# Eight more attention items with float32 score operands in an attention, gated-product and soft mixture-of-experts kernel

## The chip, the cores and the metric

The kernel runs on one core of a Trainium2 chip. The metric is the time of one execution on the device in microseconds (us), the median of three runs. The engines are TensorE (PE in the profile; its weight loads are PEld), VectorE (DVE), ScalarE (ACT), GpSimd (POOL) and SyncE (SP), which here only issues transfers.

## The reference

Three stages follow each other: causal attention with a learned decay, a product of two linear maps with two more linear maps behind it, and a soft mixture of eight experts. The change touches the first one alone, and there the line with `np.matmul(q, k...)` and the decay `bias`.

```python
batch, n_heads, seq, head_dim = (4, 8, 576, 64)
...
    scores = scale * np.matmul(q, k.transpose(0, 1, 3, 2))
    causal = np.triu(np.ones((S, S), dtype=bool), k=1)
    s_pos = np.maximum(s, 0.0)
    cum = np.cumsum(s_pos, axis=-1)
    bias = -(cum[:, :, :, None] - cum[:, :, None, :])
    scores = np.where(causal, -1000000000.0, scores + np.minimum(bias, 0.0))
    scores = scores - np.max(scores, axis=-1, keepdims=True)
    attn = np.exp(scores)
    attn = attn / (np.sum(attn, axis=-1, keepdims=True) + 1e-09)
    return np.matmul(attn, v).astype(np.float32)
...
    a = x @ w1
    b = x @ w2
    h = a * b @ w3
    return (h @ w_out).astype(np.float32)
...
    logits = x @ phi
    ...
    slot_input = d.T @ x
    ...
        h = np.maximum(slot_input[e] @ w1[e], 0.0)
        slot_out[e] = h @ w2[e]
    ...
    return (c @ slot_out).astype(np.float32)
```

## The kernel before

**Items.** Attention is cut into 40 items (`ITEMS`). Items 0 to 7 are the first three query tiles of the eight heads of batch 0, items 8 to 15 the other two tiles of the same heads, and items 16 to 39 are the heads of batches 1 to 3 with all five tiles. Items 16 to 23 are thus the eight heads of batch 1. The five query tiles have 64, 192, 320, 448 and 576 key columns; the last is cut into two halves of 288.

**Scores in two ways.** The decay is part of the product: under the 64 rows of q and k lie four rows (`rows_d` in memory, "decay rows" below) that hold the running sums of the decay, so that one product over 68 rows gives score and bias. For items below `NF32` the operands are float32: tile `raw` holds q and k in partitions 0 to 63 and the decay rows in 64 to 67, and each tile is one matmul over 68 rows. The hardware profiler records such a float32 matmul as two instructions. For items from `NF32` on, q and k are split: `raw` is loaded twice as tall (q and k stand in both halves of the partitions), VectorE casts it to `qa` (lines 311 and 313), ScalarE's queue copies 64 rows of `qa` to `qb` (312), GpSimd writes what the cast left away into the lower half of `qa` and the upper half of `qb` (317 and 314), and the SP queue loads the decay rows into `qb` (306). A tile's score is then two matmuls, one over the 128 rows of `qa` and one over the 68 rows of `qb` (line 341), both of type float32r.

**Fetching.** For items below `NF32` the tile `raw` takes its buffer from three tags in turn (`raw`, `qa`, `qb`, two buffers each), its operands are asked for four items ahead and its decay rows three items ahead (`FAR`). For the others there are two buffers of each, the operands are asked for two items ahead, and cast, subtractions and decay rows come one item ahead. `att_steps` puts these steps in the order of the items:

```python
            d = FAR if n + FAR < NF32 else 1 if NF32 <= n + 1 < N else 0
            if d:
                prep += [(0, lambda m=n + d: att_prep(m, ap))]
            d = FAR + 1 if n + FAR + 1 < NF32 else 2 if NF32 <= n + 2 < N else 0
            if d:
                prep += [(0, lambda m=n + d: att_fetch(m, ap))]
```

**What else runs there.** Behind the scores of a tile, VectorE adds the mask and takes the row minimum (344), ScalarE the exponential (349), VectorE the inverse row sums (358, 359), GpSimd multiplies by them (362), TensorE transposes (377, 391) and multiplies with the values `v` (110). Values come for two items at a time, with two buffers (290). Woven between the items are the halves of the gated product (`gl`, 439; `glu_half`), and the conversion of the weights `w12`, `wot` and `w3t` from 64-bit words: ScalarE (186, 197) and VectorE (189 to 201) convert, and small products (`wot_ps`, `w3t_ps` and their sums `wots_ps`, `w3ts_ps`) fold the weights into `u_sb` and `v_sb`, which the logits (`lg`) need.

**What sets the order.** The SP queue keeps the order in which the program issues its transfers, and a transfer whose buffer is not free holds all behind it. The order on the other engines comes from a scheduler that replays the program with costs of its own; on the chip each engine then takes its instructions strictly in that order.

Of the kernel before, what the change touches and what calls it, by code (L numbers as in the profile page):

```python
# [47 lines left out]
def attn_glu_softmoe_kernel(  # L48
# [34 lines left out]

    NW, NRAW, NG4, NX, NE_ = 8, 3, 4, 6, 11
    NRW, SCB, PTB, QAB, VB = 2, 3, 2, 2, 2
    NF32, NDIR, ND, FAR = 16, 2, 1, 3

    A1, CA, CB1, CB, GB1, GB, GC = 0.6, 8, 16, 26, 8, 16, 24

# [1028 lines left out]
```

## Time and profile before

| | |
|---|---|
| median of three runs | 566.56 us (563.37 to 568.69) |
| the profiled execution | 565.44 us |
| its span, first to last instruction | 563.6 us |
| mean granted TensorE clock | 0.981 of full speed |
| busy: TensorE, VectorE, ScalarE, GpSimd | 520.0, 316.2, 310.0, 196.7 us |

Times inside the trace count from the start of the span. "Idle before" is the time that an engine stood still before an instruction, and the name behind the arrow is what ended it; "issue" stands where the trace shows nothing that it waited for. The granted clock is a share of 2.4 GHz; 0.5 is the lower level, 1.2 GHz.

### The profile page before, as it was taken

How to read it: one execution, taken by the hardware profiler on the slowest of the kernel's cores; microseconds unless marked ns; L12 is line 12 of the kernel's file. 1: busy time of each engine (PE TensorE's matmuls, PEld its weight loads, DVE VectorE, ACT ScalarE, POOL GpSimd, SP SyncE). 2: the span in 40 equal slices, each digit the busy share in tenths (PEclk: the TensorE clock that was granted, in tenths of full speed). 3: DMA queues.
4: the chain of work that ended last, by engine and by line, in shares of the span. 5: the costliest groups of instructions: out<-in, count | busy, mean ns of one | idle time of the engine just before them, and what ended most of it. 6: DMA issues, size and time to landing. Idle time of an engine off the chain costs nothing. (4 is left out here: it accounts for less than half of the span.)

```text
span 563.6 us, 11844 instructions
## 1 busy us (share of the span) xinstructions
PE 520.0 (92%) x4288; PEld 433.9 (77%) x4288; DVE 316.2 (56%) x966; ACT 310.0 (55%) x845; POOL 196.7 (35%) x247
## 2 busy tenths in 40 slices
PE   3789899998979999899899999999999999999993
PEld 2566688787768897889889889889988999853452
DVE  7568696889964385736574657446631311243333
ACT  4576586788865675646566567357833321321222
POOL 5475464438745374253354444333210000000000
PEclk9997899999979999999999999999999999999998
DMA  5765966868654173345646563555330999689977
GB/s 157 237 179 178 261 203 215 287 219 261 191 201 119 39 220 109 130 135 179 206 136 213 168 197 104 166 167 172 113 113 1 391 413 381 233 300 421 421 296 244
DMA packets 38809, 118.03 MB, mean 209 GB/s; under 512 B 4224, under 2 KB 10560, under 8 KB 35296
## 3 DMA queue, kind: packets, MB, share of 16 engines
q1 hardware_dynamic: 36832, 113.74, 58.8%
q10 hardware_dynamic: 1920, 3.54, 2.5%
q8 instruction: 34, 0.56, 0.4%
q14 instruction: 23, 0.19, 0.1%
HBM read 102.11 MB, written 11.60 MB: 202 GB/s over the span
## 5 line engine op out<-in xcount | busy, mean ns | idle before, releaser
L439 PE MATMUL gl<-x,w12t 128*128 128x320 f32 (+1 forms) x1536 | 238.3, 304 | 1.3 <-DVE nmax L344 0.7
L439 PEld LDWEIGHTS gl<-x,w12t 128*128 128x128 f32 x1536 | 212.2, 191 | 10.0 <-issue 4.3
L362 POOL TENSOR_SCALAR sc<-sc,rinv 128x64 f32<-128x64 f32 (+4 forms) x160 | 92.4, 594 | 53.9 <-DVE rinv L359 39.2
L349 ACT ACTIVATE sc<-sc,nmax 128x64 f32<-128x64 f32 (+4 forms) x160 | 89.5, 560 | 32.2 <-DVE nmax L344 31.6
L317 POOL TENSOR_TENSOR qa<-raw,qa 64x576 fp32r<-64x576 f32 x24 | 36.5, 1522 | 144.1 <-DVE qa L311 138.3
L344 DVE CUSTOM_DVE_ANT_0 sc<-sc_ps,mask 128x64 f32<-128x64 f32 (+4 forms) x160 | 64.8, 424 | 32.1 <-PE sc_ps L341 29.0
L379 ACT COPY pt<-pt_ps 128x128 f32<-128x128 f32 (+3 forms) x128 | 52.2, 423 | 27.1 <-PE pt_ps L377 16.3
L377 PE MATMUL pt_ps<-ident,sc 128*128 128x128 f32 x320 | 56.8, 288 | 4.9 <-ACT pt L379 2.3
L341 PE MATMUL sc_ps<-qa 128*128 128x64 f32 (+1 forms) x144 | 46.6, 336 | 6.0 <-DVE nmax L344 2.5
L377 PEld LDWEIGHTS pt_ps<-ident,sc 128*128 128x128 f32 x320 | 38.8, 145 | 17.3 <-issue 10.0
L341 PE MATMUL sc_ps<-qb 68*128 68x64 f32 (+1 forms) x144 | 44.2, 310 | 4.2 <-issue 4.2
L110 PE MATMUL x_ps<-pt,v 128*64 128x256 f32 (+1 forms) x384 | 47.5, 353 | 0.0
L445 ACT COPY a<-gl 128x256 f32<-128x256 f32 (+1 forms) x64 | 25.3, 398 | 38.5 <-PE gl L439 34.8
L341 PE MATMUL sc_ps<-raw 68*128 68x288 f32 (+4 forms) x96 | 35.5, 514 | 11.1 <-DMA raw<-rows 9.6
L990 POOL MEMSET ht<- 128x1024 f32 x2 | 1.9, 954 | 107.3 <-DVE ew L894 98.4
L186 ACT ACTIVATE w_w<-raw_w 128x512 f32<-128x512 f32 x32 | 21.6, 676 | 31.6 <-DMA raw_w<-in_w 31.6
L314 POOL TENSOR_TENSOR qb<-raw,qa 64x576 fp32r<-64x576 f32 x24 | 38.2, 1590 | 2.2 <-PE gl L439 0.5
L110 PEld LDWEIGHTS x_ps<-pt,v 128*64 128x64 f32 x384 | 32.0, 138 | 6.7 <-issue 1.0
L341 PEld LDWEIGHTS sc_ps<-qa 128*128 128x128 f32 x144 | 27.7, 192 | 9.1 <-DVE nmax L344 3.5
L427 DVE TENSOR_TENSOR x<-x_ps,x 128x320 fp32r<-128x320 f32 (+1 forms) x32 | 14.0, 455 | 36.2 <-ACT x L426 36.1
L341 PEld LDWEIGHTS sc_ps<-raw 68*128 68x128 f32 x96 | 21.2, 259 | 16.3 <-issue 12.1
L341 PEld LDWEIGHTS sc_ps<-qb 68*128 68x128 f32 x144 | 28.0, 194 | 4.6 <-issue 4.4
(180 smaller groups left out, 785.4 us busy)
## 6 DMA issues: line engine op xcount, KB each, us to landing
ew<-in_ew SPq DMA_DIRECT2D x27, 1024.0 KB
raw_w<-in_w SPq DMA_DIRECT2D x32, 512.0 KB
raw<-in_qk SPq DMA_DIRECT2D x24, 576.0 KB
v<-in_v SPq DMA_DIRECT2D x16, 576.0 KB
raw_w3t<-in_w3t SPq DMA_DIRECT2D x16, 512.0 KB
raw_wot<-in_wot SPq DMA_DIRECT2D x8, 512.0 KB
raw_wo<-in_wo SPq DMA_DIRECT2D x8, 512.0 KB
w_d<-w_w SPq DMA_DIRECT2D x8, 512.0 KB
```

The source lines that it names most:

```text
L110: mm = nc.tensor.matmul(out_, lhs, rhs, start=start, stop=stop)
L186: nc.scalar.activation(out=w, in_=hi.bitcast(F32), func=AF.Copy, scale=F64_SCALE)
L314: nc.gpsimd.tensor_tensor(out=qb[0:64, 1, :q1], in0=rk[0:64, :q1], in1=qa[0:64, 1, :q1].bitcast(F32), op=ALU.subtract)
L317: nc.gpsimd.tensor_tensor(out=qa[64:, 0, q0:q1], in0=rq[64:, q0:q1], in1=qa[64:, 0, q0:q1].bitcast(F32), op=ALU.subtract)
L341: nc.tensor.matmul(pp[:r, : z - a], x[:, 0, q0 : q0 + r], x[:, 1, a:z], start=x is mul[0], stop=x is mul[-1])
L344: nc.vector.tensor_tensor_reduce(out=sc[:r, a:z], in0=pp[:r, : z - a], in1=hd["mask"][:r, m0 : m0 + z - a], scale=-0.125, scalar=3.0e38 if ...
L349: nc.scalar.activation(out=sc[:r, :W], in_=sc[:r, :W], func=AF.Exp, bias=nmax[:r, i : i + 1], scale=-1.0, accum_out=rsum[:r, i, 0:1],)
L362: nc.gpsimd.tensor_scalar(out=sc, in0=sc, scalar1=rinv[:, i : i + 1], scalar2=1.0, op0=ALU.mult, op1=ALU.mult)
L377: nc.tensor.transpose(tp[:, j * P : (j + 1) * P], sc[:, j * P : (j + 1) * P], ident)
L379: t["turned", i] = nc.scalar.copy(out=pt[:, p0 : p0 + step * (i - 1) + 1 : step], in_=tp[:, : i * P].rearrange("p (j q) -> p j q", q=P))
L439: nc.tensor.matmul(acc[:, :nt], w12_t[fc][:, wi, n, kc], x_t[b, blk, kc][:, xi], start=k == 0, stop=k == 3 * KC - 1)
L445: nc.scalar.copy(out=a_sb[:, :nt], in_=acc[:, :nt])
```

## The change

One number is changed: items 16 to 23 now take the first way, with float32 operands, and the second way begins at item 24.

```diff
-    NF32, NDIR, ND, FAR = 16, 2, 1, 3
+    NF32, NDIR, ND, FAR = 24, 2, 1, 3
```

For each of the eight items this takes away two casts on VectorE, two subtractions on GpSimd and one transfer from ScalarE's queue; it halves the load of q and k (64 rows of two operands, 288 KB, in place of 576 KB); it puts five tiles' scores of six float32 matmuls in place of twelve split ones; and operands and decay rows are asked for earlier. The scheduler then orders the engines anew from about 72 us of the profile on (in the order of before) to the scores of item 25; behind those every engine has the same order as before.

In the names below, the number behind `qa`, `qb`, `raw`, `sc` and `sc_ps` is the item, in `w3t` and `v_sb`'s source `w3ts_ps` it is the block of the weights, and `v_21` are the values of items 20 and 21.

The SP queue, around the decay rows of item 21 (`qb_21<-rows_d`), before:

```order
L306 DMA qb_20_1805<-rows_d_101 4x1152
L282 DMA raw_21_1813<-in_qk 128x2x576
L178 DMA raw_w3t_5_1_1836<-in_w3t 128x512
L178 DMA raw_w3t_6_0_1855<-in_w3t 128x512
L178 DMA raw_w3t_6_1_1919<-in_w3t 128x512
L178 DMA raw_w3t_7_0_1935<-in_w3t 128x512
L290 DMA v_21_1950<-in_v 128x1152
L306 DMA qb_21_1952<-rows_d_101 4x1152
L282 DMA raw_22_1962<-in_qk 128x2x576
```

and now, where they are loaded into `raw_21`:

```order
L306 DMA raw_21_1467<-rows_d_101 4x1152
L282 DMA raw_22_1591<-in_qk 64x2x576
L178 DMA raw_w3t_3_1_1613<-in_w3t 128x512
L178 DMA raw_w3t_4_0_1631<-in_w3t 128x512
L178 DMA raw_w3t_4_1_1680<-in_w3t 128x512
L178 DMA raw_w3t_5_0_1702<-in_w3t 128x512
L306 DMA raw_22_1591<-rows_d_101 4x1152
L282 DMA raw_23_1766<-in_qk 64x2x576
L178 DMA raw_w3t_5_1_1788<-in_w3t 128x512
L178 DMA raw_w3t_6_0_1806<-in_w3t 128x512
L178 DMA raw_w3t_6_1_1868<-in_w3t 128x512
L178 DMA raw_w3t_7_0_1883<-in_w3t 128x512
```

The decay rows of item 21 stood behind the words up to `w3t_7_0` and the values `v_21`; now they stand ahead of eight of these word loads and of `v_21`, which is the next row.

TensorE at the first score of item 21, before:

```order
L439 MATMUL gl_0_1_3_0_2050<-x_0_1_3_738,w12t_3_550 128x256 x3
L341 MATMUL sc_ps_21_0_0_2111<-qa_21_1953 128x64
L391 MATMUL ptd_ps_18_1896<-ident_86,sc_18_1594 128x128 x5
L341 MATMUL sc_ps_21_0_0_2111<-qb_21_1952 128x64
L377 MATMUL pt_ps_19_1_1971<-ident_86,sc_19_1786 128x128
L257 MATMUL w3ts_ps_3_1848<-rep_622,w3tp_3_1829 128x32
L110 MATMUL w3t_ps_4_1903<-w3t_4_1831,u_sb_106 32x128 x8
L341 MATMUL sc_ps_21_1_0_2124<-qa_21_1953 128x192
L341 MATMUL sc_ps_21_1_0_2124<-qb_21_1952 128x192
```

and now:

```order
L439 MATMUL gl_0_1_3_0_1982<-x_0_1_3_738,w12t_3_550 128x256 x3
L391 MATMUL ptd_ps_18_1845<-ident_86,sc_18_1569 128x128 x5
L341 MATMUL sc_ps_21_0_0_2043<-raw_21_1467 128x64
L377 MATMUL pt_ps_19_1_1906<-ident_86,sc_19_1748 128x128
L257 MATMUL w3ts_ps_3_1799<-rep_622,w3tp_3_1781 128x32
L110 MATMUL w3t_ps_4_1852<-w3t_4_1783,u_sb_106 32x128 x8
L341 MATMUL sc_ps_21_1_0_2055<-raw_21_1467 128x192
L341 MATMUL sc_ps_21_2_0_2066<-raw_21_1467 128x320
```

The two products of a tile, with five transposes between them in the first tile, have become one; what follows it is the same.

VectorE between the fourth tile of item 22 and the first of item 23, before:

```order
L344 ISA sc_22_2223,nmax_22_2222<-sc_ps_22_4_0_2318,mask_122 128x288
L344 ISA nmax_22_2222 128x1
L344 ISA sc_22_2223,nmax_22_2222<-sc_ps_22_4_1_2322,mask_122,nmax_22_2222 128x288
L344 ISA nmax_22_2222 128x1
L311 CAST qa_24_2437<-raw_24_2269 128x576
L313 CAST qa_24_2437<-raw_24_2269 128x576
L358 TENSOR_REDUCE rinv_22_2423<-rsum_1_94 128x5
L359 RECIPROCAL rinv_22_2423<-rinv_22_2423 128x5
L258 COPY v_sb_87<-w3ts_ps_6_2129 128x32
L457 TENSOR_TENSOR gU_0_1_4_2316<-gl_0_1_4_1_2303,a_0_1_4_2242 128x256
L258 COPY v_sb_87<-w3ts_ps_7_2205 128x32
L344 ISA sc_23_2417,nmax_23_2416<-sc_ps_23_0_0_2418,mask_122 128x64
```

and now:

```order
L344 ISA sc_22_2139,nmax_22_2138<-sc_ps_22_4_0_2222,mask_122 128x288
L344 ISA nmax_22_2138 128x1
L311 CAST qa_24_2337<-raw_24_2175 128x576
L313 CAST qa_24_2337<-raw_24_2175 128x576
L344 ISA sc_22_2139,nmax_22_2138<-sc_ps_22_4_1_2225,mask_122,nmax_22_2138 128x288
L344 ISA nmax_22_2138 128x1
L311 CAST qa_25_2475<-raw_25_2344 128x576
L313 CAST qa_25_2475<-raw_25_2344 128x576
L358 TENSOR_REDUCE rinv_22_2324<-rsum_1_94 128x5
L258 COPY v_sb_87<-w3ts_ps_6_2059 128x32
L359 RECIPROCAL rinv_22_2324<-rinv_22_2324 128x5
L457 TENSOR_TENSOR gU_0_1_4_2220<-gl_0_1_4_1_2207,a_0_1_4_2157 128x256
```

The casts of item 24 have moved ahead of the last score tile of item 22, and the casts of item 25 stand ahead of the inverse row sums of item 22 and of the copy into `v_sb`.

## Rows read from the trace of the kernel before

**Rows 1.** Page, busy us, share of the span and instructions of an engine.
```profile
PE 520.0 (92%) x4288; PEld 433.9 (77%) x4288; DVE 316.2 (56%) x966; ACT 310.0 (55%) x845; POOL 196.7 (35%) x247
```

**Rows 2.** Stretches: busy us of PE, PEld, DVE, ACT, POOL; TensorE's clock, DMA.
```profile
98.00:168.00 70.00, 62.06 (x549) 52.31 (x547) 59.84 (x155) 55.05 (x147) 37.33 (x37) 0.95 0.73 237
98.00:200.00 102.00, 93.88 (x856) 79.42 (x855) 74.18 (x215) 73.50 (x203) 53.77 (x57) 0.97 0.60 190
200.00:480.00 280.00, 272.41 (x2263) 249.78 (x2262) 140.29 (x439) 152.49 (x423) 86.97 (x114) 1.00 0.54 186
161.00:167.00 6.00, 5.79 (x39) 5.15 (x40) 5.31 (x16) 4.81 (x15) 3.16 (x2) 0.56 0.42 144
```

**Rows 3.** Waits of PE from 98 to 200 us: total, times, longest.
```profile
PE sc_ps L341 <- issue: 4.2, 1, 4.2
PE sc_ps L341 <- DVE nmax L344: 1.1, 1, 1.1
```

**Rows 4.** Timeline of PE at 156 us: start, length, what [idle before].
```profile
156.21 0.20 PE L341 MATMUL sc_ps<-qa 128*128 128x64 f32 x1
156.24 0.75 PE L391 MATMUL ptd_ps<-ident,sc 128*128 128x128 f32 x5
161.21 0.39 PE L341 MATMUL sc_ps<-qb 68*128 68x64 f32 x1 [4.21 <-issue]
```

**Rows 5.** Timeline of the SP queue, 140 to 157 us.
```profile
142.78 9.93 SPq L178 DMA_DIRECT2D raw_w3t<-in_w3t  x4
...
153.28 0.28 SPq L306 DMA_DIRECT2D qb<-rows_d  x1
```

**Rows 6.** Timeline of POOL, 147 to 149.5 us.
```profile
147.22 1.75 POOL L314 TENSOR_TENSOR qb<-raw,qa 64x576 fp32r<-64x576 f32 x1
```

**Rows 7.** Timeline of PE, float32 scores at full clock, 34 to 43 us.
```profile
35.16 1.33 PE L341 MATMUL sc_ps<-raw 68*128 68x64 f32 x6
36.37 0.41 PE L377 MATMUL pt_ps<-ident,sc 128*128 128x128 f32 x2
...
39.75 1.89 PE L341 MATMUL sc_ps<-raw 68*128 68x448 f32 x6
41.48 0.49 PE L391 MATMUL ptd_ps<-ident,sc 128*128 128x128 f32 x3
```

**Rows 8.** Timeline of PE, split scores of item 17, 118 to 130 us.
```profile
120.68 0.19 PE L341 MATMUL sc_ps<-qa 128*128 128x64 f32 x1
...
121.20 1.73 PE L110 MATMUL x_ps<-pt,v 128*64 128x256 f32 x16
...
123.56 0.39 PE L341 MATMUL sc_ps<-qa 128*128 128x320 f32 x1
...
123.94 1.24 PE L439 MATMUL gl<-x,w12t 128*128 128x256 f32 x9
...
125.02 0.37 PE L341 MATMUL sc_ps<-qa 128*128 128x448 f32 x1
...
125.70 0.28 PE L439 MATMUL gl<-x,w12t 128*128 128x256 f32 x1
...
126.85 0.38 PE L341 MATMUL sc_ps<-qa 128*128 128x288 f32 x1
...
127.21 0.38 PE L377 MATMUL pt_ps<-ident,sc 128*128 128x128 f32 x2
```

**Rows 9.** Groups by form, DVE and POOL: busy us, mean ns | idle before.
```profile
L311 DVE CAST qa<-raw 128x576 fp32r<-128x576 f32 x24 | 11.7, 486 | 5.0 <-issue 2.1 <-PE sc_ps L341 1.4 <-DMA raw<-in_qk 1.3
...
L314 POOL TENSOR_TENSOR qb<-raw,qa 64x576 fp32r<-64x576 f32 x24 | 38.2, 1590 | 2.2 <-PE gl L439 0.5
```

**Rows 10.** Line 198 on DVE: duration min/median/max in ns, first and last start.
```profile
L198 DVE SCALAR_TENSOR_TENSOR w3t<-w3t,raw_w3t x16: 653/692/1927, 110.4 to 167.0; 128x512 int32<-128x512 int32 x16
```

**Rows 11.** Timelines of the SP queue and of DVE, 176 to 184 us.
```profile
176.85 0.68 SPq L282 DMA_DIRECT2D raw<-in_qk  x1
...
182.98 0.46 DVE L311 CAST qa<-raw 128x576 fp32r<-128x576 f32 x1 [2.11 <-issue]
```

## Prediction, made before the changed kernel ran

> **What bounds the kernel now.** I read first the share of time that each engine is busy, then the same by stretches, then what ended TensorE's idle time, and only then single instructions. TensorE is busy 92% of the span and no other engine is over 56% [rows 1]. The eight items that the change touches take their scores from 108 to about 197 us. In the 102 us from 98 to 200 us TensorE is busy 93.9 us, VectorE 74.2, ScalarE 73.5 and GpSimd 53.8 [rows 2]: TensorE sets the pace here too, and only 8.1 us of it is idle. More than half of that is one wait of 4.2 us, for which the trace can name no releaser; the next longest is 1.1 us, ended by VectorE [rows 3].
>
> The long wait is part of the code that the change removes. At 156.2 us TensorE runs the 64 wide product of item 21 from `qa`, then five transposes, and the second product, from `qb`, starts only at 161.2 [rows 4]. GpSimd had finished its part of that `qb` at 149.0 (147.22 + 1.75) [rows 6]. What is left to come late is the part that the SP queue loads, the four decay rows of item 21. SP was held for 9.9 us at four loads of `w3t` words, each waiting for its buffer, so the decay rows were issued at 153.3 only, behind words and values [rows 5]. After the wait the granted clock is 0.56 from 161 to 167 us, the lower of its two levels (1.2 GHz) for most of it [rows 2].
>
> **Part 1, scores from float32: a cost on TensorE.** Eight items lose 12 products of split operands and get 6 in float32 (each recorded as two instructions). Price at full clock, from the start of one group to the start of the next thing on the engine. Float32: the first three query tiles took 36.37 - 35.16 = 1.21 us, and 448 + 288 + 288 columns took 41.48 - 39.75 = 1.73, together 2.94 us an item [rows 7]. Split, item 17: 121.20 - 120.68 = 0.52, 123.94 - 123.56 = 0.38, 125.70 - 125.02 = 0.68 and 127.21 - 126.85 = 0.36, together 1.94 us [rows 8]. So +1.00 us an item, **+8.0 us**. All of it lies on the engine that sets the end, with nothing beside it to hide it. I take it as the upper end. Should some of TensorE's busy time be pipeline fill between the short products, which longer ones cover, it is less: the 64 and 192 wide products take 0.52 us for 256 columns, the 320 wide ones 0.38, so the small tiles pay mostly for something other than columns; half of it, 4.0, is my lower end.
>
> The Trainium skill (FP8 and Floating Point Precision, TensorE Precision Notes) says "True FP32: 4 passes through PE array". By that rule, against two products of one pass each, an item of 1,600 columns would pay two passes more, an estimate of 2 x 1600 / 2.4 GHz = 1.33 us, or 10.7 us for eight. The trace agrees for float32 (2.94 us against 2.67) but not for the split products, which take 1.94 and not 1.33. With that price the sum below would come out 2.7 us higher.
>
> **Part 2, the long wait: a gain.** In the new order the decay rows of item 21 are queued three items ahead, before eight `w3t` loads that used to stand in front of them, and into the tile that the raw operands already lie in. Nothing is then left between two products of a tile that could come late. Gain: 4.2 us of idle time, and what half speed cost after it: 6 us at 0.56 lose 6 x 0.44 = 2.6 us [rows 2], of which some 0.1 was idle; I take 2.5. Together **-6.7 us**. Bounds: 0 if something else is late at the same place, 6.7 if not. Late next are the `w3t` products that follow at once. Their words were there in the trace of before when TensorE came to them, and by item 21 TensorE has five dearer items behind it, some 5 us less the waits that go, while the words come no later. So I take the full gain.
>
> **Part 3, less on VectorE and GpSimd: a small gain.** Gone are 16 casts of about 0.5 us on VectorE (8 us), and on GpSimd 16 subtractions of about 1.6 us (25 us) [rows 9], 8 transfers from the ScalarE queue, and half of each raw load (288 instead of 576 KB). None of these engines sets the pace, so their busy time is worth nothing by itself. What counts are TensorE's other waits in the stretch, 8.1 - 4.2 = 3.9 us, mostly on results of VectorE [rows 3]. With 8 us less in its queue, and fewer of the conversions that took 1.9 instead of 0.69 us [rows 10], I give back half: **-2.0 us**, between 0 and -3.9.
>
> **Part 4, the switch to split operands moves from item 16 to item 24: a small cost.** Whatever comes first with split operands has its raw data fetched only when the prefetched items are done. On VectorE the casts of items 24 and 25 now both stand before the row sums of item 22 and the copy into `v_sb` that the logits wait for; before, only the casts of 24 did. Before, VectorE waited there 2.1 us for the raw operands of 24, issued at 176.85 and cast at 182.98, 6.1 us later [rows 11]. Now it also waits for those of 25, asked for right after. Count from the moment when the values' buffer is free and SP goes on. The raw operands of 24 are asked for 0.8 us later and cast from 6.9 to 7.8; those of 25 come 0.8 us behind them if the loads overlap, 3 us (half of 6.1, which values and operands took together) if they queue. I take 2: from 8.9, cast by 9.8, copy at 10.2. TensorE comes to the logits at 9.6: about 5.0 us of work to its last score of item 22, then logits, transposes, a `w3t` group and a GLU half of together 4.6, by the timeline of the same stretch. That is **+0.6 us**, bounded by 0 and, when a whole load's wait falls on TensorE, 6.1 us. Queued behind the waiting casts are VectorE's evictions of GLU halves and scores, and for those TensorE's four `sg` buffers wait.
>
> **The sum.** +8.0 - 6.7 - 2.0 + 0.6 = -0.1 us. Behind item 25 the order of all engines is the same as before, and TensorE is 97% busy (272.4 of the 280 us from 200 to 480) [rows 2], so what is won or lost by 200 us stays to the end. The profiled execution took 565.44 us (span 563.6 and 1.8 around it); with the sum it is **565.3 us**. The median of the runs is 566.56, 1.1 higher, inside their own spread of 5 us; on that base the same sum gives 566.5.
>
> **Rivals.**
> - *The wait comes back at the switch.* If VectorE's wait for the raw operands of items 24 and 25 runs TensorE dry as item 21 did, the price is again a wait of some 4.2 us and 2.5 us at half clock, in place of the 0.6: 565.3 - 0.6 + 6.7 = 571.4 us, slower by 1%; with the wait at its bound of 6.1 us and the same clock after it, 573.3. It decides once the raw loads of 24 and 25 take over about 9 us from issue to cast. For it: the fetch of 24 still waits behind the values of items 22 and 23, whose buffer is freed by products of items 18 and 19. Against it: TensorE had work queued through the 6.1 us in the trace of before and did not stop.
> - *VectorE is the true pacer here.* From 98 to 168 us it is busy 59.8 of 70 us, with TensorE's long wait in the same stretch [rows 2]. Beside GpSimd's subtractions a conversion takes 1.93 us instead of 0.69 [rows 10]; if that goes, the words and evictions all come early, and every wait of TensorE in the stretch goes. TensorE's own work is the floor: 93.9 - 2.5 + 8.0 = 99.4 us in place of 102, so -2.6 us: 562.8 us. If at the same time only half of part 1 is paid (4.0), it is 558.8, faster by 1.2%. The Trainium skill (SBUF — State Buffer, "SBUF: two separate sides") has the rule for it: VectorE with two operands in SBUF and a GpSimd instruction lock each other out of a shared port pair for a whole instruction. By that rule all 16 subtractions taken away are time that VectorE gets back; the trace agrees, with its 1.93 and 0.69 us, on single conversions.
> - *Nothing is won back.* TensorE pays the 8.0, and at item 21 the `w3t` words turn out late instead, so that only parts 3 and 4 count: 565.44 + 8.0 - 2.0 + 0.6 = 572.0 us. Against it speaks that words were ahead of TensorE.
> That the change does not do what it says is not among them: the instruction order shows the eight items' scores read from `raw` alone.
>
> **How the numbers follow.** A measurement of this kernel can tell about 1%, 5.7 us, from no change. My forecast, with its bounds on parts 1 and 3 (one at a time, some 561 to 568 us), gets 0.65, and all of that lies within 1%. The wait at the switch gets 0.10 and nothing won back 0.08, both slower by about 1%. VectorE as pacer gets 0.17, of which 0.11 with the longer, faster end. So: faster 0.12, same 0.70, slower 0.18 (a little of the forecast's tails goes to either side). The range leaves out one in ten on each side: 560.5 to 571.5 us.
>
> **What would show each step.** Part 1: eight more items with float32 products at 0.48 to 0.49 us for 288 columns and 0.75 for 448, and TensorE's busy time up by 5 to 8 us. Part 2: no wait over 1 us on TensorE before item 24, and a granted clock of 1.0 from 100 to 200 us. Part 3: VectorE's busy time down by 8 us and more, GpSimd's by about 25, conversions near their 0.69 us. Part 4: TensorE's idle time where items 22 to 25 meet, under 1 us. The forecast is wrong if the float32 products push other work on TensorE into waits that I don't see, or if the new order of the stretch from 72 us on, which also moves GLU halves and transposes, opens a wait of its own.

## The result, and the profile after

The changed kernel takes 570.98 us (median of 14 runs, 568.28 to 576.57); the kernel before, run beside it, 566.64 us (14 runs). The ratio is 1.0107, with a 95% interval from 1.0079 to 1.0135: slower by about 1%. Medians are of all runs; the ratios leave out runs that took over 1.5% longer than the shortest of their kernel, and so differ a little from the ratios of the medians. In a later set of runs the same two kernels stood at 573.17 and 564.75 us, ratio 1.014 (1.0106 to 1.0174). The forecast was 565.3 us, no change.

The profiled execution took 571.08 us, its span is 569.3. The first view is the page's busy time of the changed kernel, to be read against [rows 1].

```profile
PE 531.5 (93%) x4288; PEld 439.7 (77%) x4288; DVE 303.5 (53%) x950; ACT 312.0 (55%) x845; POOL 168.9 (30%) x231
```

VectorE has lost 12.7 us of busy time and GpSimd 27.8, somewhat more than the 8 and 25 of the prediction, and TensorE has 11.5 more. The next view gives stretches of the changed kernel with the columns of [rows 2].

```profile
98.00:200.00 102.00, 98.32 (x832) 78.95 (x831) 61.15 (x194) 71.91 (x195) 31.77 (x47) 1.00 0.48 154
200.00:480.00 280.00, 272.73 (x2244) 250.05 (x2243) 141.04 (x448) 153.22 (x428) 84.21 (x109) 0.99 0.52 181
```

TensorE is fuller from 98 to 200 us (98.3 busy instead of 93.9) and at full clock, VectorE and GpSimd are emptier, and yet the stretch gets longer. The long wait is gone, as the timeline of TensorE at item 21 shows (start, length, what, as in [rows 4]): one float32 product takes the place of two, and nothing stands idle ahead of it or behind it.

```profile
161.41 0.71 PE L391 MATMUL ptd_ps<-ident,sc 128*128 128x128 f32 x5
161.96 0.33 PE L341 MATMUL sc_ps<-raw 68*128 68x64 f32 x2
162.13 0.28 PE L377 MATMUL pt_ps<-ident,sc 128*128 128x128 f32 x1
```

**Where the time went.** I cut each profile at two places that all kernels here have: the first products of `ptd` with the values at about 72 us, where the order of the engines begins to differ, and the first score of item 26, behind which it no longer does. Ahead of this stretch the two profiles of each kernel spread by themselves (72.95 and 70.13 us before, 72.73 and 74.16 after). Behind it, to the end of the span, they agree: 339.4 and 340.3 us before, 340.7 and 340.1 after. So the loss that belongs to the change lies inside. The windows of that stretch, length, TensorE busy, its clock, DMA, first of the two profiles of before (the second is the run `before_again` below), then of the two of after:

```profile
72.95:224.24 151.29, 143.05 (x1235) 0.98 0.58 187
```

```profile
70.13:222.16 152.03, 144.00 (x1234) 0.98 0.58 187
```

```profile
72.73:228.57 155.84, 150.38 (x1235) 1.00 0.51 160
```

```profile
74.16:231.41 157.25, 150.10 (x1235) 1.00 0.52 158
```

The changed kernel needs 4.6 and 5.2 us more. Below, "idle" is the length less the busy time, "clock" is what TensorE's work lost while it ran at 1.2 GHz (half of the time that it ran there), and "work" is the busy time less that loss.

| stretch from 72 us to item 26 | length | work | idle | clock |
|---|---|---|---|---|
| before, two profiles | 151.3, 152.0 | 140.5, 141.2 | 8.2, 8.0 | 2.5, 2.8 |
| after, two profiles | 155.8, 157.3 | 150.4, 150.1 | 5.5, 7.2 | 0, 0 |

Work went up by 9.4 us on average, the clock gave back 2.7, and idle time only 1.8. The waits of TensorE in the stretch, of after (total, times, longest):

```profile
PE sc_ps L341 <- DVE gT L457: 1.0, 1, 1.0
PE gl L439 <- DVE nmax L344: 0.9, 2, 0.7
PE lg L110 <- DVE v_sb L258: 0.8, 1, 0.8
PE wots_ps L257 <- ACT wotp L249: 0.6, 1, 0.6
PE pt_ps L377 <- POOL sc L362: 0.6, 1, 0.6
...
PE dt_ps L586 <- ACT pt L379: 0.4, 1, 0.4
```

They come to 5.2 us. Three of them stand where the split operands now begin ("the switch"): the logits' wait of 0.8 us that part 4 foresaw, and two behind it, which TensorE's timeline shows.

```profile
186.76 0.73 PE L110 MATMUL lg<-gC,v_sb 128*32 128x320 f32 x2 [0.81 <-DVE v_sb L258]
...
215.13 0.55 PE L586 MATMUL dt_ps<-ident,lT 128*128 128x128 f32 x3 [0.37 <-ACT pt L379]
...
217.85 1.43 PE L439 MATMUL gl<-x,w12t 128*128 128x320 f32 x8 [0.70 <-DVE nmax L344]
```

The second profile of after has the same three with 0.80, 0.37 and 0.71 us; neither profile of before has any of them. The first of the three comes from VectorE, which copies into `v_sb` only behind the casts of item 25. VectorE's two casts, and the subtraction of item 24 that GpSimd runs beside the second:

```profile
184.14 0.81 DVE L311 CAST qa<-raw 128x576 fp32r<-128x576 f32 x1 [0.37 <-DMA raw<-in_qk]
184.86 1.67 DVE L313 CAST qa<-raw 128x576 fp32r<-128x576 f32 x1
```

```profile
184.70 1.51 POOL L314 TENSOR_TENSOR qb<-raw,qa 64x576 fp32r<-64x576 f32 x1
```

The operands of item 25 were only 0.37 us late. The casts took 0.81 and 1.67 us, where those of item 24 took 0.46 and 0.45; the difference, 1.6 us, is more than the logits' wait. The second profile has 0.18 us of waiting and casts of 0.99 and 1.67 us.

The other waits are 3.3 us in the first profile of after and 5.2 in the second. Before they were 3.8 and 5.1 beside the wait at item 21. In sum they did not shrink, but what ends them changed: of the listed waits, those ended by VectorE fell from 2.5 and 3.7 us to 1.2 and 0.7, those ended by ScalarE and GpSimd rose from 1.3 and 1.4 to 2.1 and 4.5. VectorE did get faster. Its conversions of `w3t`, 73 to 200 us, before and after (busy us, mean ns, idle time ahead of them and what ended it):

```profile
L198 DVE SCALAR_TENSOR_TENSOR w3t<-w3t,raw_w3t 128x512 int32<-128x512 int32 x16 | 15.6, 979 | 2.1 <-ACT raw_w3t L197 2.1
L201 DVE SCALAR_TENSOR_TENSOR w3t<-raw_w3t,w3t 128x512 int32<-128x512 int32 x16 | 14.4, 899 | 0.1
```

```profile
L201 DVE SCALAR_TENSOR_TENSOR w3t<-raw_w3t,w3t 128x512 int32<-128x512 int32 x16 | 11.8, 735 | 0.1
L198 DVE SCALAR_TENSOR_TENSOR w3t<-w3t,raw_w3t 128x512 int32<-128x512 int32 x16 | 11.4, 714 | 10.2 <-ACT raw_w3t L197 10.0 <-ACT w3t L186 0.2
```

These 32 conversions took 6.8 us less, and VectorE then stood 10.0 us instead of 2.1 at ScalarE's half of the same words. The second profiles agree (979 and 910 ns before, 747 and 739 after, with 2.0 and 9.9 us at ScalarE). What VectorE won it spent waiting. ScalarE in turn stands longer at the words themselves, by its waits from 73 to 200 us, before and after (total, times, longest):

```profile
ACT w3t L186 <- DMA raw_w3t<-in_w3t: 4.9, 7, 1.4
```

```profile
ACT w3t L186 <- DMA raw_w3t<-in_w3t: 7.4, 7, 2.1
```

And the words come no earlier in the end. In the changed kernel SP is done with the words up to `w3t_7_0` sooner, but then stands 9.9 us at the load of the values `v_21`, whose buffer the products with the values free (its wait there ends at `x_ps` on TensorE). The last word behind it was issued at 157.6 us, before the change at 155.5:

```profile
138.72 8.07 SPq L178 DMA_DIRECT2D raw_w3t<-in_w3t  x4
156.71 0.33 SPq L290 DMA_DIRECT2D v<-in_v  x1
157.09 0.33 SPq L306 DMA_DIRECT2D raw<-rows_d  x1
157.58 0.33 SPq L178 DMA_DIRECT2D raw_w3t<-in_w3t  x1
```

This is read from the trace; no run moves the values to another queue.

### The profile page after: what moved, and what is told of

The parts are those of the page before. It is cut to its first block, busy times and chain, and to the rows that moved or that the text cites. A ratio compares the mean times of both kernels' runs of the same rounds, so it can differ in the third digit from the quotient of the medians.

```text
span 569.3 us, 11741 instructions
## 1 busy us (share of the span) xinstructions
PE 531.5 (93%) x4288; PEld 439.7 (77%) x4288; DVE 303.5 (53%) x950; ACT 312.0 (55%) x845; POOL 168.9 (30%) x231
## 4 chain that ended last, share of the span: by engine, by line
PE 37%; DMA 5%; DVE 4%; ACT 2%; issue 1%; POOL 1%; SPq 0%; DVEq 0%; POOLq 0%; ACTq 0%
PE gl L439 17%; DMA raw_w<-in_w 5%; PE x_ps L110 3%; PE o_ps L1019 3%; PE h_ps L981 3%; PE gn_ps L609 2%; PE sc_ps L341 2%; PE pt_ps L377 1%; PE z_ps L110 1%; DVE w_w L198 1%; PE y_ps L905 1%; PE lg L110 1%; PE ptd_ps L391 1%; DVE sc L344 1%; DVE w_w L201 1%
## 5 line engine op out<-in xcount | busy, mean ns | idle before, releaser
L439 PEld LDWEIGHTS gl<-x,w12t 128*128 128x128 f32 x1536 | 213.2, 191 | 11.1 <-issue 5.5
L362 POOL TENSOR_SCALAR sc<-sc,rinv 128x64 f32<-128x64 f32 (+4 forms) x160 | 89.3, 576 | 109.9 <-DVE rinv L359 66.9
L341 PE MATMUL sc_ps<-raw 68*128 68x288 f32 (+4 forms) x192 | 64.0, 462 | 12.0 <-DMA raw<-rows 9.6
L317 POOL TENSOR_TENSOR qa<-raw,qa 64x576 fp32r<-64x576 f32 x16 | 24.7, 1542 | 119.4 <-DVE qa L311 113.7
L341 PEld LDWEIGHTS sc_ps<-raw 68*128 68x128 f32 x192 | 37.1, 229 | 20.6 <-issue 14.8
L110 PEld LDWEIGHTS x_ps<-pt,v 128*64 128x64 f32 x384 | 34.4, 142 | 7.3 <-issue 2.1
L341 PE MATMUL sc_ps<-qa 128*128 128x64 f32 (+2 forms) x96 | 30.5, 331 | 3.8 <-DVE gC L457 2.3
L612 ACT COPY gn<-gn_ps 128x512 f32<-128x512 f32 x40 | 22.6, 584 | 14.6 <-PE gn_ps L609 14.2
L349 ACT ACTIVATION_READ_ACCUMULATOR sc<-sc,nmax 128x1 f32 x160 | 30.6, 191 | 0.0
L110 PE MATMUL x_ps<-ptd,v 128*64 128x64 f32 x320 | 29.4, 238 | 0.3 <-ACT ptd L393 0.3
L341 PE MATMUL sc_ps<-qb 68*128 68x64 f32 (+2 forms) x96 | 29.3, 308 | 0.0
```

The source lines that it names most:

```text
L110: mm = nc.tensor.matmul(out_, lhs, rhs, start=start, stop=stop)
L317: nc.gpsimd.tensor_tensor(out=qa[64:, 0, q0:q1], in0=rq[64:, q0:q1], in1=qa[64:, 0, q0:q1].bitcast(F32), op=ALU.subtract)
L341: nc.tensor.matmul(pp[:r, : z - a], x[:, 0, q0 : q0 + r], x[:, 1, a:z], start=x is mul[0], stop=x is mul[-1])
L349: nc.scalar.activation(out=sc[:r, :W], in_=sc[:r, :W], func=AF.Exp, bias=nmax[:r, i : i + 1], scale=-1.0, accum_out=rsum[:r, i, 0:1],)
L362: nc.gpsimd.tensor_scalar(out=sc, in0=sc, scalar1=rinv[:, i : i + 1], scalar2=1.0, op0=ALU.mult, op1=ALU.mult)
L439: nc.tensor.matmul(acc[:, :nt], w12_t[fc][:, wi, n, kc], x_t[b, blk, kc][:, xi], start=k == 0, stop=k == 3 * KC - 1)
```

## The experiments

Times are medians. Of the kernel before, run beside each set, they were 564.75 us (first set), 565.02 (second), 565.46 (third) and 566.21 (fourth). Two theories go through them. *A*: TensorE's work counts in full, and so does every wait taken from it. *F*: a little below today's time there is a floor, set by VectorE, ScalarE and the words together, so that work or waits taken from TensorE come back as other waits. "The stretch" is the one measured above, 151.3 and 152.0 us before, 155.8 and 157.3 after. A change of `NF32` or of TensorE's products also lets the scheduler order the engines anew, and no run holds that order fixed.

**First set: the wait alone, work alone, and the scores made cheap**

`rows_from_act`, against before:

```diff
-            nc.sync.dma_start(rows[64:68, :, :q1].bitcast(F32), ...)
+            (nc.sync if n < NF32 else nc.scalar).dma_start(rows[64:68, :, :q1].bitcast(F32), ...)
```

> The kernel before, with all its split items, but their decay rows are issued from ScalarE's queue instead of the SP queue, so that they no longer stand behind the w3t words. It does part 2 of the prediction alone. Theory A (the 4.2 us wait at item 21 is these four rows behind the words, and with the half clock after it is worth 6.7 us): no wait over 1.5 us on TensorE before item 24, time 566.6 - 6.7 = 560 us, between 558 and 562. Rival (something else is late at the same place, the words or the values): a wait of 2 to 4 us stays near item 21, or comes up a few us later, and the time is within 2 us of before, 565 to 568.

569.65 us, ratio 1.0091 (1.0057 to 1.0124). A falls as a statement on this kernel, but two things are mixed. In the stretch the wait named "issue" is gone and 1.4 and 2.1 us are won (149.9 us). From item 26 on the kernel is some 8 us longer than before: the decay rows of items 24 to 39 on ScalarE's queue open waits of their own there. The run `rows_16_23` keeps them apart.

`qa_twice`, against before:

```diff
-            for x in mul:
+            for k, x in enumerate((mul[0], *mul) if 16 <= n < 24 else mul, -(16 <= n < 24)):
-                nc.tensor.matmul(..., start=x is mul[0], stop=x is mul[-1])
+                nc.tensor.matmul(..., start=x is mul[0], stop=x is mul[-1] or k < 0)
```

> The kernel before, but in items 16 to 23 the product over qa is run twice, the second run overwriting the first: about as much more TensorE work as the change adds (six products of 0.19 to 0.39 us, some 1.0 us an item, 8 us in all), with the casts, subtractions, transfers and order of loads of before. Theory A (TensorE's own time counts in full wherever it is put): the wait at item 21 is shortened by what TensorE has to do before it, by at most 4.2 us, so the time is 566.6 + 8 less 0 to 6.7, 568 to 574.6. If all of it is taken up by waits: 566.6. A number above 572 says that the wait moves along with the work.

565.23 us, ratio 0.9996 (0.9965 to 1.0027): below A's range, no measurable cost. The window of the stretch:

```profile
71.66:225.80 154.14, 147.31 (x1282) 0.99 0.57 186
```

The 48 products put 5 us of work on TensorE, not 8 (147.3 less 1.7 for the clock is 145.6, against 140.5 and 141.2). The wait at item 21 is gone without anything having been done about it: TensorE now comes there at 164.2 us, behind the decay rows, which were issued at 154.7. Part of that is the new order, in which item 20 too has its first score at 153.0 us instead of 143.4. So the wait of before was room that other work can fill, and float32 scores did not have to remove it to be paid from it. In this profile the stretch is 2 to 3 us longer; the median shows nothing.

`cheap_scores`, against after:

```diff
-            t["mul"] = [rows[:68]]
+            t["mul"] = [rows[:68].bitcast(mybir.dt.bfloat16)[:, :, 1::2] if n >= 16 else rows[:68]]
```

> The changed kernel, but items 16 to 23 take their scores from the upper 16 bits of each float32 operand, read as bfloat16 in place: the low 16 bits of q, k and decay rows of those eight items are left out of the computation, everything that is loaded, and the arrangement around it, stays. Six products of one pass, about 1 us an item in place of the 2.94 us in float32. Theory A (the float32 products are the cost, paid in full): 571 - 8 x 1.95 = 555.4 us, between 553.5 and 558. Rival B (the price shows up elsewhere: the waits and clock falls behind item 24 at about 243 and 283 us): those falls stay where they are and the gain is 12 us or less, 559 or more. Rival C (VectorE or the loads set the pace in these items once TensorE is cheaper): waits on TensorE from 100 to 200 us grow by several us, 560 to 566.

564.23 us, ratio to before 0.9984 (0.9957 to 1.0012). Against after it wins 7 to 9 us where A wanted 15.6. The window of the stretch, and under it the three longest of TensorE's waits there:

```profile
71.43:220.08 148.65, 135.69 (x1187) 1.00 0.55 168
```

```profile
PE lg L110 <- DVE v_sb L258: 3.1, 1, 3.1
PE ptd_ps L391 <- ACT pt L379: 2.8, 2, 2.4
PE gl L439 <- ACT a L445: 1.3, 1, 1.3
```

TensorE's work is 14.6 us below that of after, the stretch only 7.2 and 8.6. The rest is idle time, 13.0 us of it. The largest piece, the logits' wait for `v_sb`, is the switch again: VectorE's copy stands behind the casts of item 25, which wait 2.47 us for their operands.

```profile
179.28 0.47 DVE L311 CAST qa<-raw 128x576 fp32r<-128x576 f32 x1 [2.47 <-DMA raw<-in_qk]
179.68 1.65 DVE L313 CAST qa<-raw 128x576 fp32r<-128x576 f32 x1
181.25 0.18 DVE L258 COPY v_sb<-w3ts_ps 128x32 f32<-128x32 f32 x1
```

Of the other 9.3 us of listed waits, 7.3 end at ScalarE. That speaks for F, and for rival C of the expectation: no run here has this stretch under 148.6 us. That one and the same limit stands behind each of them is not shown.

`after_again`, the changed kernel unchanged:

> The changed kernel once more, for a second profile of it. If the two stretches at half clock at about 243 and 283 us, after waits of 2.0 and 1.5 us that the kernel before has too, belong to the change, they stand in this profile as well, and the profiled execution takes about 571 us. If they come and go between executions, this profile has one of them or none, each worth some 1.6 us, and the time is 568 to 571 us.

573.17 us. Of the two stretches at half clock behind item 24 only the one at 283 us is there, the one at 243 us is not. The second expectation holds for them, though the profiled execution took 573.3 us, longer than it gave; the run gave the second profile used above.

**Second set: the wait alone again, and the number of items**

`rows_16_23`, against before:

```diff
+            (nc.scalar if 16 <= n < 24 else nc.sync).dma_start(rows[64:68, :, :q1].bitcast(F32), ...)
```

> The kernel before, with the decay rows of items 16 to 23 alone issued from ScalarE's queue; items 24 to 39 load theirs from the SP queue as before. In the run in which all split items did it, the stretch from 72 us to item 24 took 124.7 us instead of 126.7 although the 4.2 us wait was gone, and items 24 to 39 lost 10 us. Theory A (the wait at item 21 is worth its whole 6.7 us): 565 - 6.7 = 558 us. Theory F (a floor: with that wait gone other waits, on VectorE's evictions and on the words, come up in its place, and 2 to 3 us are left): 562 to 563 us, with waits of over 1 us ended by VectorE between 120 and 165 us. Items 24 to 39 as before in both, 202.6 us from the first score of item 24 to that of item 39.

561.38 us, ratio 0.9939 (0.9908 to 0.997): faster than both kernels, and F rather than A. TensorE at item 21 and just behind it:

```profile
153.93 0.20 PE L341 MATMUL sc_ps<-qa 128*128 128x64 f32 x1
153.97 0.28 PE L341 MATMUL sc_ps<-qb 68*128 68x64 f32 x1
...
159.80 0.41 PE L341 MATMUL sc_ps<-qa 128*128 128x320 f32 x1 [2.02 <-DVE nmax L344]
```

The product from `qb` now follows at once, so the late part was the four decay rows, as the prediction said. But 6 us later, in the same item, TensorE waits 2.0 us for VectorE. And the clock still falls twice in the stretch, at 141 and at 161 us. The stretch takes 149.9 us: idle time is down by 2 us, to 5.9, and the clock still costs 3.4. Taking the wait away by itself is worth 3.6 us by the medians, not 6.7.

`nf20`, against before; `nf28` and `nf40` have 28 and 40 in the same place:

```diff
-    NF32, NDIR, ND, FAR = 16, 2, 1, 3
+    NF32, NDIR, ND, FAR = 20, 2, 1, 3
```

> Half of the change: items 16 to 19 from float32 operands, 20 to 23 split. Theory A (float32 costs 1.0 to 1.1 us an item, in full, and the wait goes only where the decay rows of item 21 are moved ahead of the words): 565 + 4.3 less what of the wait at item 21 is filled by later arrival, at most 4.2 and the 2.5 of half clock: 563 to 569 us, likeliest 566. Theory F (in this stretch TensorE has up to 7 us of slack that any work fills): 565 or 566 too; the two differ in the wait at item 21, which A leaves at 3 us or more and F at less than 1.

571.17 us, ratio 1.0117 (1.0062 to 1.0172), above what both theories gave. The wait at item 21 is gone, which F foresaw. The profiled execution (568.26 us) is one of its two shortest; in it the stretch is 152.5 us, about that of before, with 3.6 us more work on TensorE and less idle time. So this profile does not say where the rest of the 6 us lies. By the medians half of the change costs as much as the whole of it, which neither theory explains; this stays open.

> The change and four items more: items 24 to 27 from float32 operands too. There TensorE is busy 95 to 97 of 100 us and there is no long wait to fill. Theory A: 4 x 1.08 = +4.3 us over the changed kernel, 571 to 573 becomes 575 to 577. Rival (what the change loses behind item 24 is the switch to split operands, which the words and the logits of batch 0 make dear, and it is cheaper four items later): 571 to 573, no more than after.

572.62 us, ratio 1.0101 (1.006 to 1.0141): the number is the rival's. Four more items in float32 add nothing that can be measured to the 571 and 573 us of the change. Its profiled execution is the shortest of twelve (565.09 us), so its total says little. The logits' wait is absent in it, and so are the two behind it; the stretch, with the float32 scores of items 24 and 25 in it, is as long as in after (155.9 us).

> All items from float32 operands, no split ones left: no casts, subtractions or copies, no switch. Theory A: 16 x 1.08 = 17.3 us over the changed kernel's 571 to 573, less the 3 us or so that the switch and the waits behind it cost there: 585 to 588. Rival (part 3 of the prediction after all: with VectorE and GpSimd relieved, TensorE's waits in batches 2 and 3, some 8 us, shrink too): 578 to 582.

587.48 us, ratio 1.0407 (1.0355 to 1.046): here A has the number. From the first score of item 26 to that of item 39, the windows of this kernel and of before:

```profile
228.04:419.20 191.16, 186.17 (x1422) 1.00 0.39 124
```

```profile
224.24:401.05 176.81, 169.92 (x1417) 1.00 0.49 159
```

TensorE has 16.3 us more work and the thirteen items take 14.4 us longer, 1.1 an item. In batches 2 and 3, where TensorE is busy 169.9 of 176.8 us and the longest wait is 2.1 us, nearly all of the price is paid; 1.9 us come out of idle time.

**Third set: a second profile of before, the switch, and the other direction**

`before_again`, the kernel before unchanged:

> The kernel before once more, for a second profile. In its first one the stretch from item 24 to 39 had waits of 2.06 and 1.45 us without a fall of the clock behind them; the two profiles of the changed kernel have two and one falls there, 1.7 us each. If the falls go with the execution and not with the change, this profile has one or two of them there too, and the time is 563 to 567 us with the 4 us wait at item 21 again. If the change makes them, there are none.

565.60 us. The wait at item 21 is there with 2.5 us, followed by another 1.2 us and the low clock; and behind the wait of 1.5 us at 275 us the clock falls in this profile, as it did not in the first:

```profile
157.00:165.00 8.00, 6.41 (x53) 0.65 0.53 192
```

```profile
275.00:279.00 4.00, 3.66 (x18) 0.57 0.99 295
```

So the stretches at half clock behind item 26 go with the execution, not with the change. A reading of the first pair of profiles alone, that the change loses 3 us by them, would be wrong.

`after_early`, against after:

```diff
-            d = FAR + 1 if n + FAR + 1 < NF32 else 2 if NF32 <= n + 2 < N else 0
-            if d:
-                prep += [(0, lambda m=n + d: att_fetch(m, ap))]
+            m0 = {21: (24,), 22: (25,), 23: ()}
+            for m in m0.get(n, (n + FAR + 1,) if n + FAR + 1 < NF32 else (n + 2,) if NF32 <= n + 2 < N else ()):
+                prep += [(0, lambda m=m: att_fetch(m, ap))]
```

> The changed kernel, with the raw operands of items 24 and 25 asked for one item earlier, so that VectorE's casts at the switch no longer wait for them. Theory S (the switch costs 0.8 us at the logits, and then 2.0 us between the scores of items 24 and 26, because VectorE is late): the waits at 187, 215 and 218 us go, items 24 to 26 take 25.8 to 26.7 us instead of 27.8, and the time is 2 to 3 us below the changed kernel, 568.5 to 570. Rival (what is lost there is the order of the products and evictions, not the late operands): 571 to 573, with the waits at 215 and 218 us as they were.

572.19 us, ratio to before 1.0125 (1.0071 to 1.0179), no better than after, so rather the rival; the interval, 569.5 to 575.6 us, still touches theory S. From 180 to 235 us the waits of TensorE are these two:

```profile
PE dt_ps L586 <- ACT pt L379: 0.7, 1, 0.7
PE lg L110 <- DVE nmax L344: 0.3, 1, 0.3
```

The logits' wait for `v_sb` is gone: with the operands there earlier, item 24 is cast at 171 us, so that only the casts of item 25 are left ahead of the copy. A wait of the `dt_ps` transposes stays, so that part of what is lost behind the switch belongs to the new order of products and evictions. The profiled execution was the longest of its six (577.91 us), so its length is not compared; but from the first score of item 24 to that of item 26 it takes 26.4 us, between after (27.7 and 27.9) and before (25.7 twice), as theory S had it. Why that does not show in the median stays open.

`nf8_rows`, against before, with `rows_16_23`'s line from item 8 on:

```diff
-    NF32, NDIR, ND, FAR = 16, 2, 1, 3
+    NF32, NDIR, ND, FAR = 8, 2, 1, 3
+            (nc.scalar if 8 <= n < 24 else nc.sync).dma_start(rows[64:68, :, :q1].bitcast(F32), ...)
```

> The other way: items 8 to 15 (two query tiles each) take split operands too, and the decay rows of items 8 to 23 are issued from ScalarE's queue. By the prices of the prediction such an item has 1.73 us of products in float32 and 1.04 in split operands, so TensorE saves 8 x 0.69 = 5.5 us. Theory A (TensorE's work counts in full): 561.4 - 5.5 = 556 us. Theory F (with less on TensorE, and 16 casts and 16 subtractions more in the stretch with the most words, waits open instead, as with the cheap scores, where half of the saving was lost): 558.5 to 563 us.

579.65 us, ratio 1.0271 (1.0213 to 1.033): both theories miss, F by the less. From 60 to 220 us TensorE's waits are led by these:

```profile
PE sc_ps L341 <- DVE nmax L344: 5.5, 5, 2.0
PE ptd_ps L391 <- ACT pt L379: 3.3, 3, 2.0
PE gl L439 <- DVE gC L457: 2.1, 2, 1.5
```

Here the preparation of split operands, or with it the issues on ScalarE's queue, which this run adds for items 8 to 15 too, costs TensorE far more in waits than the products save; the two were not tried apart. Float32 operands, which lose in items 16 to 23, win in items 8 to 15.

**Fourth set: the removed work put back, and another queue for the rows**

`prep_both`, against after; `prep_dve` has the first loop alone, `prep_pool` the second:

```diff
+            if n >= 16:
+                for k in range(2):
+                    nc.vector.tensor_copy(rows[0:64, k, :q1], rows[0:64, k, :q1])
+                for k in (1, 0):
+                    for lo, hi in ((0, 320), (320, q1)):
+                        nc.gpsimd.tensor_tensor(out=rows[0:64, k, lo:hi], in0=rows[0:64, k, lo:hi], in1=hd["mask"][0:64, : hi - lo], op=ALU.add)
```

> The changed kernel, with work put back on VectorE and GpSimd that the change took away: for each of items 16 to 23 two copies of 64 x 576 in place on VectorE, and on GpSimd two additions of zero of that size, each in two pieces; all values stay as they are. Theory N (part 3 of the prediction is worth nothing, this work was never in TensorE's way): within 1.5 us of the changed kernel, 570 to 574, TensorE idle 4 to 6 us from the products of batch 0 at 73 us to item 24. Rival (part 3 holds: 2 us or more were won back and lost elsewhere): 574 to 577, with 2 to 4 us more of waits in that stretch.

585.17 us, ratio to before 1.0359 (1.0319 to 1.0398): theory N falls, and the rival's 577 is passed too. The window of the stretch, and under it, by form, a conversion and the copies on VectorE from 73 to 200 us:

```profile
72.18:241.00 168.82, 157.74 (x1235) 0.95 0.49 147
```

```profile
L198 DVE SCALAR_TENSOR_TENSOR w3t<-w3t,raw_w3t 128x512 int32<-128x512 int32 x16 | 16.1, 1006 | 1.3 <-ACT raw_w3t L197 1.2 <-ACT w3t L186 0.2
...
L310 DVE COPY raw<-raw 64x576 f32<-64x576 f32 x16 | 8.9, 587 | 5.6 <-DMA raw<-in_qk 5.1 <-issue 0.5
```

TensorE is idle 11.1 us in the stretch and loses 7.9 to the clock, which in the changed kernel cost nothing there; its work is the same. The conversions are about as slow as before the change. This is not quite the removed work. The copies stand 5.1 us at loads that in the changed kernel no engine but TensorE waits for, and GpSimd's additions take 34.0 us where the change had taken away 27.8.

> The same with the two copies an item on VectorE alone. Theory N: 570 to 574. If VectorE is what TensorE waits for here, most of what the run with both engines shows is in this one.

571.80 us, ratio to before 1.0123 (1.007 to 1.0176): N. VectorE's copies alone cost nothing by the medians. The profile is of one of its two longest executions (576.38 us); in it the stretch is 162.0 us, with 10.2 us idle, so that the median may hide a cost that only some executions have.

> The same with the GpSimd additions alone, some 25 us of GpSimd in the stretch, beside VectorE's evictions. Theory N: 570 to 574. If GpSimd's work slows VectorE's (1.93 instead of 0.69 us for a conversion, as the trace of before shows once), waits on VectorE grow here as much as with the copies, and the time goes above 574.

576.17 us, ratio to before 1.018 (1.0144 to 1.0216): 3 to 5 us above the changed kernel. The two kinds of work together cost 12 to 14 us, far more than the sum of one by one. The conversions take 906 and 826 ns again beside GpSimd's additions, although VectorE has nothing more to do itself; with VectorE's copies alone they took 719 and 722.

`rows_pool`, against before:

```diff
+            (nc.gpsimd if 16 <= n < 24 else nc.sync).dma_start(rows[64:68, :, :q1].bitcast(F32), ...)
```

> The kernel before, with the decay rows of items 16 to 23 issued from GpSimd's queue: the same removal of the wait at item 21 as from ScalarE's queue (561.4 us), without its cost on ScalarE. Theory F (what is left of the 6.7 us is set by the other engines, not by who issues the rows): 561 to 563 us. Theory A (the issues on ScalarE ate the rest): 557.5 to 560.

564.05 us, ratio 0.9978 (0.9946 to 1.0011), above what both theories gave and not clear of no gain at all. The wait at item 21 is gone here too, and waits ended by VectorE stand in its place (2.8 us ahead of scores, 2.0 ahead of a GLU half). The stretch takes 149.6 us, with 8.0 us idle as before the change and nothing lost to the clock. So moving the issues off ScalarE does not give the rest of the 6.7 us: nearer to F.

## Why the prediction was wrong

The sum missed by 5 us: -0.1 us forecast, 4.6 and 5.2 measured in the stretch. By its own steps, first pair of profiles and second; part 3 is what idle time is left when the wait at item 21 and the three waits at the switch are taken out:

| step | forecast | measured |
|---|---|---|
| part 1, work on TensorE | +8.0 | +9.9, +8.9 |
| part 2, the wait | -4.2 | -4.2, -2.5 |
| part 2, the clock behind it | -2.5 | -2.5, -2.8 |
| part 3, TensorE's other waits | -2.0 | -0.5, -0.3 |
| part 4, the switch | +0.6 | +1.9, +1.9 |
| sum | -0.1 | +4.6, +5.2 |

**The step that failed is part 3**: "I give back half: -2.0 us". It measured -0.5 and -0.3. Parts 1 and 4 were sized 1.4 and 1.3 us too low on average and weigh nearly as much; there the cost was foreseen, here the gain did not come. Every sign that the prediction named for part 3 did: VectorE's 13 us and GpSimd's 28 us went, the conversions came at 714 and 735 ns. TensorE's waits for VectorE, those at the switch aside, shrank too, by 1.3 and 3.0 us, about what was forecast. But waits that end at ScalarE or GpSimd (`wotp`, `sc`, `a`, `pt`) took most or all of that up, and VectorE stood 8 us longer at ScalarE's conversions. The signs did not include TensorE's waits in sum, and [rows 3], with one wait for VectorE in it, says nothing of who comes next. `cheap_scores` shows that there is such a next limit: with 14.6 us less work TensorE was idle 13.0 us, of which 3.1 belong to the switch and most of the rest end at ScalarE. Which of ScalarE and the words sets it was not tried apart.

The work put back shows that the relief was not worth nothing either: with float32 scores and like work back on VectorE and GpSimd the kernel takes 585 us. How much of the 12 to 14 us is the work, how much the loads that it then waits for and how much the clock, which falls more there, stays open.

**Part 4** had its place right, and its first size by luck (0.6 forecast, 0.8 measured at the logits). It had VectorE wait 1.1 us for the operands of item 25 (from 7.8 to 8.9) and cast them in 0.9; the wait was 0.4 and 0.2 us and the two casts took 2.5 and 2.7 us, the longer one beside a subtraction on GpSimd. And it stopped counting there. Two more waits, 1.1 us together, stand some 30 us later, between items 25 and 26. I took the point from which the order is the same as the end of the change; it ends where the last wait does that the new order brings.

**Part 1** was 8.0 "as the upper end", and 9.4 came on average. By TensorE's timeline, from each start to the next less idle time and low clock, the score products of the stretch went from 26.3 and 26.5 us to 33.5 and 33.4, about 7 more and within the price. Most of the rest stands at the products of the GLU halves: these, in the same number, went from 53.6 to 55.0, which prices taken from scores alone can't show. It is not peculiar to float32: in `qa_twice`, with more products from split operands, they take 54.7, and 53.9 with cheap scores. The Trainium skill (FP8 and Floating Point Precision, TensorE Precision Notes) counts four passes for float32, from which the prediction estimated 10.7 us; the 9.4 us lie between that and my price, the score products alone below both.

**Part 2** held: the decay rows were what came late, and moving them ahead of the words took both wait and low clock away. But the same removal without float32 work gave 3.6 us from ScalarE's queue and 2.2 from GpSimd's, by the medians, and 5 us of work without the removal cost nothing that can be measured. A stall filled by work is not the same as a stall removed; in these runs the 6.7 us came in full only where part 1 stood beside them.

**What is won or lost stays to the end** held from item 26 on, within 1.3 us.

Of the rivals, two came near in their numbers, 571.4 and 572.0, by mechanisms that were not there. *The wait comes back at the switch* would have a wait of over 4 us and half clock there; the three waits come to 1.9 us at full clock. *Nothing is won back* has the words late at item 21, which they were not. *VectorE is the true pacer* is half right. Its time of 562.8 is far off, but TensorE's waits for VectorE did shrink, and VectorE's and GpSimd's work put back together does make the kernel slower.

## What to carry to other kernels

Where the bound engine is 92% busy, look for what it would wait for next before crediting relief elsewhere: here no run brought the stretch more than 3 us or so below its time of before, and what VectorE and a removed stall freed was mostly taken up by other waits. Name the sum of the bound engine's waits as the sign of such a gain, not the busy time of the engine that is relieved. A stall on the bound engine can pay for added work, but only once. The version to keep is the old kernel with one line changed, the decay rows of items 16 to 23 issued from ScalarE's queue: 561.4 us, 0.6% faster than before.

## What the runs showed of the hardware

Subtractions or additions of two operands on GpSimd slow VectorE's conversions: 979 and 899 ns on average beside the subtractions, 714 and 735 without them, 906 and 826 with additions put back on GpSimd and VectorE's own work left as it was. The Trainium skill (SBUF — State Buffer, "SBUF: two separate sides") has the two engines lock each other out of a port pair; the runs agree with it, in the mean of 32 instructions and not only in single ones.

The clock behind the same wait falls in one execution and not in the next: after 1.45 us of idle time at 276 us it stayed at 2.4 GHz in the first profile of before, after 1.50 us at the same product it went to 1.2 GHz in the second. A difference of one or two such stretches between two profiles, some 1.7 us each, is no finding before a second profile of the same kernel has it too.
